# A spectral filter and a Fourier mixing layer in one kernel: new tiling of A's transform, of the slots, of B's input and of the matrix comparison

## The chip, the cores and the metric

One core of a Trainium2 chip runs the whole kernel. Its engines are PE (TensorE, matrix multiplication), DVE (VectorE), ACT (ScalarE), POOL (GpSimd) and SP (SyncE, which here only issues DMAs). Each engine works through its own list of instructions in order; semaphores join the lists. The metric is the device time of one execution in microseconds; less is better. The time before is 275.98 us, the median of three runs (274.37 to 276.39).

## The reference

Two independent layers are computed in float32 and set side by side along the last axis. S is 2048, D is 512.

```python
def _A_ref(x, w_r, w_i):
    X = rfft2(x, axes=(-2, -1))
    return irfft2(X * (w_r + 1j * w_i), s=(S, D), axes=(-2, -1))

def _B_ref(x, dft_seq_re, dft_seq_im, dft_hid_re, dft_hid_im):
    a = einsum("bsd,ed->bse", x, dft_hid_re)
    b = einsum("bsd,ed->bse", x, dft_hid_im)
    return einsum("ts,bse->bte", dft_seq_re, a) - einsum("ts,bse->bte", dft_seq_im, b)

out = concatenate([_A_ref(...), _B_ref(...)], axis=-1)
```

B's matrices are inputs: two of 2048 x 2048 (16.8 MB each) and two of 512 x 512. The kernel computes B by a fast transform, which is right only if these matrices are the Fourier matrices. So it also reads them whole and compares them with tables; if they differ, a fallback (`_b_from_c`) computes B again with the matrices as they are.

## The kernel before, in words

There are three strands of work. Python generators (`a_work`, `b_work`, `all_compared`) emit them, two lists of numbers (`B_AT`, `C_AT`) say between which steps of A the steps of B and C are emitted, and a scheduler then sets the final order of each engine.

**A, the filter.** `forward` loads x in eight pieces of 512 KB (SP), forms sums and differences of mirrored halves (DVE, `TT`, 16 of 512 elements), transforms the hidden axis in groups (PE, `hidden`: eight matmuls 256 wide for each of eight groups; the weights are every 16th column), copies to SBUF (ACT, `taken`, L489), does a first small transform along the sequence (PE, `along`: two matmuls 512 wide) and copies again (ACT, L496). Now the sequence has to become the partition. This turn goes through DRAM: POOL issues 16 DMAs of 256 KB into `out_a` as scratch (L498), and SP reads them back into `zv` in eight DMAs of 512 KB. Eight `slot`s then follow, one per residue of the sequence frequency: sums and differences (DVE), two matmuls (`px`), two multiplications of 1024 by the weights, sums and differences again, eight matmuls (`pi`, L455 with `it`) and two ACT copies back into `zv` (L600). The first frequency column is repaired by small operations on POOL (L531, L532, L581, L582), and ACT flips a sign in the weights (L521). `inverse` is two stages: 64 matmuls 256 wide out of `zv` with ACT copies (L619), then 64 matmuls 256 wide out of those with ACT copies (L630), and four stores of 1 MB.

**B, the mixing layer.** x_b is loaded in eight pieces of 512 KB of 64 partitions each, so that partition p and its mirror stand together. `b_fold` adds and subtracts mirrored columns (DVE, 8 operations of 1024). `b_along` transforms groups of 16 rows (PE, 128 matmuls of 128 or 72 columns; three ACT copies per group). `b_hidden` transforms the hidden axis (nine times, five matmuls each), `b_rows` the rest of the sequence (eight times). Each row block goes out twice, by a direct and an indirect DMA, both issued by POOL (L442, L443).

**C, the comparison.** `compare` loads 64 blocks of 512 KB of the matrices into three buffers (`raw`, SP, L323) and, for each, writes the difference to the table `tt` in bfloat16 (`diff`, DVE, L309 with a sign per partition or L311). ACT then takes the absolute value of each pair and sums it (L302, 34 of 2048 elements). The sum is compared with a threshold (L711), SP reads the flag, and a branch decides on the fallback.

PE has one list for all three, and so has DVE; all matmuls of A are recorded at L455 and all tensor_tensor operations of DVE at L226, whatever emits them.

Of the kernel before, what the change touches and what calls it, by code (L numbers as in the profile page):

```python
# [18 lines left out]
YB = 2  # L19
RAW = 3  # L20


B_AT = [4, 10, 10, 12, 12, 14, 14, 14, 14, 15, 15, 15, 15, 17, 19, 19, 19, 19, 26, 28, 30, 32, 35, 38, 40, 42]
C_AT = [0, 0, 0, 0, 0, 0, 0, 0, 0, 0, 0, 0, 0, 0, 0, 0, 0, 0, 0, 0, 0, 6, 6, 6, 6, 6, 35, 35, 35, 35, 35, 35, 35, 35, 35, 35, 35, 35, 35, 35, 35, 35, 35, 35, 35, 35, 35, 35, 37, 37, 37, 37, 37, 37, 37, 37, 37, 37, 37, 37, 37, 37, 37, 37, 37, 37, 37, 37]
SMALL = 2.0**-27

# [26 lines left out]
def _seq_order():  # L55

    j = np.arange(64)
    return ((128 * np.arange(16)[:, None, None] + np.stack([j, -1 - j])) % S).reshape(-1)
# [8 lines left out]
def _tables_b():  # L67
# [22 lines left out]

    rows = _b_rows()
# [25 lines left out]
    return fb.reshape(2, 128, 128).transpose(1, 0, 2), mb, hc  # L117


def _tables():  # L120
# [17 lines left out]
    inv = fwd.transpose(0, 3, 2, 1)  # L138
    inv0 = (fwd0 * np.array([1, 1, -1, -1])[:, None, None, None]).transpose(3, 0, 2, 1)

    th = _ang(np.outer(np.arange(S // 2), np.arange(513)), S)
    tt = np.stack([np.cos(th), -np.sin(th)]).reshape(2, 4, 2, 128, 513).transpose(1, 0, 3, 2, 4)
# [3 lines left out]
    fb, mb, hc = _tables_b()  # L146
    j = np.arange(128)
    place = np.stack([j, np.where(j, 256 - j, 128)])
# [6 lines left out]
    a = np.arange(8)[:, None] + 8 * np.arange(2)  # L155
    f16 = np.zeros((8, 2, 8, 16, 8))
    for k in range(16):
        th = _ang(a * (k // 2), 16)
        re, im = (np.cos(np.pi * a) if k == 1 else np.cos(th)), -np.sin(th)
        top, low = (re, re) if k < 2 else (im, -re) if k % 2 else (re, im)  # L160
        for n in range(4):
            f16[:, :, n, k, n] = f16[:, :, 4 + n, k, n] = top
            f16[:, :, n, k, 4 + n] = low
            f16[:, :, 4 + n, k, 4 + n] = -low
    back = np.where((np.arange(16) % 2 == 1) & (np.arange(16) > 1), -1.0, 1.0)[:, None, None, None, None]
    g16 = (f16.transpose(3, 4, 1, 0, 2) * back).reshape(128, 128)
    g16 = np.concatenate([g16, -g16], 1)

    di = np.zeros((128, 2, 2, 2, 128))
    for h in range(2):  # L170
# [8 lines left out]
    turn = (S - _b_rows()).T % S  # L179
    turn[0, 0] = S // 2  # L180
    return {
        "fwd": fwd.reshape(7, 128, 128).astype(np.float32),
        "fwd0": fwd0.reshape(4, 128, 128).transpose(1, 0, 2).reshape(128, 512).astype(np.float32),
        "inv": inv.reshape(7, 128, 128).astype(np.float32),
        "inv0": inv0.reshape(128, 512).astype(np.float32),
        "hf": hf.reshape(2, 128, 512).transpose(1, 0, 2).astype(np.float32),
        "f16": f16.reshape(128, 128).astype(np.float32),
        "g16": g16.astype(np.float32),
        "di": di.reshape(128, 1024).astype(np.float32),
        "tt": tt.astype(np.float32),  # L190
        "ht": ht.astype(np.float32),
        "odd": odd.astype(np.float32),
        "fb": fb.astype(np.float32),
# [7 lines left out]
def kernel(  # L201
# [13 lines left out]

# [7 lines left out]
    def STT(*args, **kw):  # L228
        last[0] = nc.vector.scalar_tensor_tensor(*args, **kw)

# [3 lines left out]

    ap = first.enter_context(tc.tile_pool(name="ap", bufs=1))
    bp = first.enter_context(tc.tile_pool(name="bp", bufs=1))  # L240
    rp = first.enter_context(tc.tile_pool(name="rp", bufs=2, side="right"))
# [3 lines left out]
    def region(name):  # L245

        return ap.tile([P, 8208 if name == "big" else 8192], F32, name=name)

    def part(v, kb, *shape):

        v = v[:, 256 * kb : 256 * kb + math.prod(shape)]
        if len(shape) == 1:
            return v
        names = "abcde"[: len(shape)]
        return v.rearrange("p (%s) -> p %s" % (" ".join(names), " ".join(names)), **dict(zip(names, shape)))
# [3 lines left out]
    ht = bp.tile([P, 2, 2, 257], F32, name="ht")  # L259
    hc = bp.tile([P, 2, 257], F32, name="hc")  # L260
    fb = bp.tile([P, 2, 8, 16], F32, name="fb")
    mb = bp.tile([P, 1409], F32, name="mb")
    ye = bp.tile([P, 2304], F32, name="ye").rearrange("p (j c s) -> p j c s", c=2, s=9)
    yo = bp.tile([P, 128, 25], F32, name="yo")
    stat = bp.tile([P, 34], F32, name="stat")
    ones = bp.tile([P, P], F32, name="ones")
    odd = bp.tile([P, 2], F32, name="odd")
    turn = bp.tile([P, 8], mybir.dt.int32, name="turn")
    nc.gpsimd.dma_start(turn, tabs["turn"])
    nc.vector.memset(ones, 1.0)  # L270

    zero = bp.tile([P, 2, 1024], mybir.dt.bfloat16, name="ec", bufs=2)[:, 0, :512]
    nc.vector.memset(zero, 0.0)
    warm = ps_a.tile([P, 2, 512], F32, name="pa")
    for _ in range(9):
        nc.tensor.matmul(warm[:, 0], zero[:, :P], zero, start=True, stop=True)

    loads = []

    def load(dst, src):  # L280
        loads.append(nc.sync.dma_start(dst, src))
        return dst

    def late(dst, src):

        with tc.issue_after(loads[-1].ins):
            nc.sync.dma_start(dst, src)

    tt, hts = {}, []
    pin = [None]  # L290

    def table(pr, m):

        if (pr, m) not in tt:
            tt[pr, m] = bp.tile([P, 2, 513], F32, name="tt", bufs=3)
            nc.sync.dma_start(tt[pr, m], tabs["tt"][pr, m])
        return tt[pr, m]

    def compared(i, d):

        flat = d.rearrange("p m i -> p (m i)")
        nc.scalar.activation(flat, flat, mybir.ActivationFunctionType.Abs, accum_out=stat[:, i : i + 1])  # L302

    def diff(out, raw, v, flip, sign):

        with tc.issue_after(pin[0].ins) if pin[0] is not None else ExitStack():
            if sign is not None:
                k = int(sign != flip)
                nc.vector.scalar_tensor_tensor(out, v, odd[:, k : k + 1], raw, op0=MUL, op1=SUB)  # L309
            else:  # L310
                nc.vector.tensor_tensor(out=out, in0=raw, in1=v, op=ADD if flip else SUB)  # L311

    def compare():

        i = 0
        for pr in (0, 4, 1, 5, 2, 6, 3, 7):
            for tb in range(4):
                d = bp.tile([P, 2, 1024], mybir.dt.bfloat16, name="ec", bufs=2)
                for m in range(2):
                    t = table(pr % 4, m)  # L320
                    v = t[:, :, 512:0:-1] if tb % 2 else t[:, :, :512]
                    raw = bp.tile([P, 2, 512], F32, name="raw", bufs=RAW)
# [8 lines left out]
                    if m == 1:  # L331
                        compared(i, d)
                        i += 1
                    yield 1.2

    def hidden_table():

# [494 lines left out]
```

## Time and profile before

| what | value |
|---|---|
| time, median of 3 runs | 275.98 us |
| the profiled execution: span from first to last instruction | 276.3 us |
| granted TensorE clock, mean | 0.850 |
| PE, DVE, ACT, POOL busy | 211.5, 161.2, 136.0, 42.8 us |
| DMA | 73.85 MB, mean 267 GB/s |
| matmuls of the first stage of the inverse | 195.90 to 226.4 us |
| flag written | 270.25 us |

The profile is one execution recorded by hardware. The span is the profiled execution's own time; it is 0.1% over the median of the runs. A row of the grouped lines reads: line, engine, operation, output and inputs with their shapes, count, then busy time, mean ns of one, and the idle time of the engine ahead of these instructions with what ended it. A row of a timeline reads: start, duration, engine, line, operation, count, and in brackets the idle time before it and its releaser. A row of the stretches reads: the stretch, busy time and count for PE, PE's weight loads, DVE, ACT and POOL, the granted clock, the share of the DMA engines and GB/s. A row of the chain reads: start, duration, what. An f32 matmul leaves two records on PE, so x16 there are eight instructions.

### The profile page before, as it was taken

What the parts mean: (1) busy time and instruction counts of PE and PEld (TensorE: products, weight loads), DVE (VectorE), ACT (ScalarE), POOL (GpSimd) and SP (SyncE); (2) the same over time, 40 slices, a digit from 0 to 9 for tenths busy, and PEclk for the clock granted to TensorE, in tenths of its full rate; (3) what the DMA queues carried; (4) which work ended last, traced back from release to release, by engine and by line L of the source; (5) the groups of instructions that cost most, each with busy time, mean ns of one, the idle gap of its engine ahead of it and who ended that gap; (6) DMA issues with size and microseconds to landing.
All of it is one profiled execution on the core that took longest, in us unless ns stands there. A gap on an engine that the chain in (4) does not pass through costs nothing.

```text
span 276.3 us, 2713 instructions
## 1 busy us (share of the span) xinstructions
PE 211.5 (77%) x833; PEld 169.0 (61%) x833; DVE 161.2 (58%) x225; ACT 136.0 (49%) x219; POOL 42.8 (15%) x80
## 2 busy tenths in 40 slices
PE   5049999299878799999999676302999995999630
PEld 1039788177678358787875445002799994876520
DVE  0860001685748359797968679745485754675340
ACT  1001430649866251856337235415678775774570
POOL 3000120013210016250213333013010100000000
PEclk9658999899955599999999797755599999899795
DMA  7999999889995998585844343775979888889763
GB/s 256 403 243 214 215 379 418 293 267 343 354 401 181 367 399 311 193 248 194 289 145 109 141 161 103 288 250 208 284 250 332 298 259 294 273 279 369 287 264 126
DMA packets 27460, 73.85 MB, mean 267 GB/s; under 512 B 2928, under 2 KB 9072, under 8 KB 26928
## 3 DMA queue, kind: packets, MB, share of 16 engines
q1 hardware_dynamic: 24432, 64.48, 70.5%
q0 software_dynamic: 2720, 8.56, 8.2%
q10 hardware_dynamic: 288, 0.59, 0.7%
q8 instruction: 8, 0.13, 0.2%
q14 instruction: 12, 0.10, 0.1%
HBM read 61.03 MB, written 12.58 MB: 266 GB/s over the span
## 4 chain that ended last, share of the span: by engine, by line
DMA 48%; PE 24%; DVE 13%; issue 8%; ACT 4%; SPq 1%; POOL 0%; DVEq 0%; POOLq 0%; ACTq 0%
DMA raw<-in_cm 23%; PE pa L455 12%; DMA ht<-tab_ht 6%; DMA out_b<-yb,turn 6%; DMA big<-in_xb 6%; DVE ec L309 5%; PE pb L414 4%; DVE ec L311 3%; PE pb L412 3%; DMA zv<-in_xa 2%; DMA zv<-out_a 2%; ACT ec L302 2%; DMA out_b<-yb 2%; DVE yb L226 2%; DVE sda L226 2%
## 5 line engine op out<-in xcount | busy, mean ns | idle before, releaser
L302 ACT ACTIVATE ec<-ec 128x2048 bf16<-128x2048 bf16 x34 | 65.0, 1911 | 33.4 <-DVE ec L311 21.8
L311 DVE TENSOR_TENSOR ec<-raw,tt 128x512 bf16<-128x512 f32 (+1 forms) x48 | 40.0, 865 | 51.7 <-DMA raw<-in_cm 51.6
L309 DVE SCALAR_TENSOR_TENSOR ec<-tt,odd,raw 128x512 bf16<-128x512 f32 (+1 forms) x48 | 42.5, 926 | 19.2 <-DMA raw<-in_cm 18.9
L455 PE MATMUL pa<-zb,sda 128*128 128x256 f32 x128 | 32.2, 410 | 12.2 <-DVE sda L226 12.2
L455 PEld LDWEIGHTS pa<-zb,sda 128*128 128x128 f32 x128 | 30.4, 307 | 15.5 <-DVE sda L226 13.1
L455 PE MATMUL pa<-ye,sda 128*128 128x256 f32 x128 | 32.2, 414 | 6.5 <-ACT zb L630 3.4
L455 PEld LDWEIGHTS pa<-ye,sda 128*128 128x128 f32 x128 | 26.4, 208 | 12.2 <-ACT zb L630 4.6
L455 PE MATMUL pa<-it,sda 128*128 128x128 f32 x112 | 19.2, 339 | 17.9 <-POOL sda L581 16.0
L455 PEld LDWEIGHTS pa<-it,sda 128*128 128x128 f32 x112 | 17.9, 246 | 23.6 <-POOL sda L581 20.1
L455 PE MATMUL pa<-ye,zv 128*128 128x256 f32 x128 | 30.5, 403 | 0.7 <-ACT zv L600 0.7
L455 PEld LDWEIGHTS pa<-ye,zv 128*128 128x128 f32 x128 | 29.3, 306 | 1.8 <-ACT zv L600 1.0
L226 DVE TENSOR_TENSOR sda<-zv 128x512 f32<-128x512 f32 x30 | 19.5, 687 | 15.4 <-DMA zv<-in_xa 7.5
L226 DVE TENSOR_TENSOR sda<-sda 128x512 f32<-128x512 f32 (+1 forms) x34 | 23.0, 717 | 0.3
L489 ACT COPY zb<-pa 128x1024 f32<-128x1024 f32 x8 | 8.1, 1007 | 28.5 <-PE pa L455 28.5
L226 DVE TENSOR_TENSOR sda<-pa,sda 128x1024 f32<-128x1024 f32 (+1 forms) x16 | 17.7, 1151 | 5.6 <-ACT sda L557 3.9
L455 PE MATMUL pa<-zb 128*128 128x512 f32 x32 | 16.6, 645 | 5.5 <-ACT zb L489 5.5
L397 PE MATMUL pb<-fb,yb 128*128 128x72 f32 x64 | 14.5, 319 | 3.1 <-ACT ye L403 3.1
L397 PEld LDWEIGHTS pb<-fb,yb 128*128 128x128 f32 x64 | 13.1, 248 | 6.2 <-ACT ye L403 4.0
L397 PE MATMUL pb<-fb,big 128*128 128x128 f32 (+1 forms) x64 | 16.5, 351 | 0.0
L498 POOL DMA_DIRECT2D out_a<-zb x16 | 8.5, 534 | 49.5 <-ACT zb L496 49.3
L429 ACT COPY yb<-pb 128x514 f32<-128x514 f32 x8 | 4.7, 587 | 19.4 <-DMA out_b<-yb,turn 17.1
L397 PEld LDWEIGHTS pb<-fb,big 128*128 128x128 f32 x64 | 13.1, 251 | 1.0 <-issue 1.0
(78 smaller groups left out, 247.0 us busy)
## 6 DMA issues: line engine op xcount, KB each, us to landing
raw<-in_cm SPq DMA_DIRECT2D x64, 512.0 KB, 4.9
tt<-tab_tt SPq DMA_DIRECT2D x8, 513.0 KB, 10.3
zv<-in_xa SPq DMA_DIRECT2D x8, 512.0 KB, 8.6
big<-in_xb SPq DMA_DIRECT2D x8, 512.0 KB, 16.1
out_a<-zb POOLq DMA_DIRECT2D x16, 256.0 KB, 6.2
sda<-in_wa SPq DMA_DIRECT2D x16, 256.0 KB, 3.4
zv<-out_a SPq DMA_DIRECT2D x8, 512.0 KB, 8.7
out_a<-zb SPq DMA_DIRECT2D x4, 1024.0 KB, 6.9
```

Source lines behind the costliest of these rows:

```text
L226: last[0] = nc.vector.tensor_tensor(**kw)
L302: nc.scalar.activation(flat, flat, mybir.ActivationFunctionType.Abs, accum_out=stat[:, i : i + 1])
L309: nc.vector.scalar_tensor_tensor(out, v, odd[:, k : k + 1], raw, op0=MUL, op1=SUB)
L311: nc.vector.tensor_tensor(out=out, in0=raw, in1=v, op=ADD if flip else SUB)
L397: nc.tensor.matmul(bank[:, at : at + n].rearrange("p (j s) -> p j s", j=8), v[:, cols], f[:, :, k], start=True, stop=True)
L412: nc.tensor.matmul(out, yo[0:1, :, at[1]], hc[0:1, 1], start=False, stop=True)
L414: nc.tensor.matmul(bank[:, 257:], yo[:, :, at[2] + 16 * c], ht[:, c, 1, 1:256], start=c == 0, stop=c == 1)
L429: nc.scalar.copy(y[:, :, :257], bank[:, :257].unsqueeze(1).to_broadcast([P, 2, 257]))
L455: mma[0] = nc.tensor.matmul(*args, **kw)
L489: nc.scalar.copy(zs[p], pd[p])
L498: nc.gpsimd.dma_start(bounce[:, 2 * p + k], ys[:, k])
```

## The change

Everything but the launch and the fallback is written anew.

- **A's x and the turn.** x_a goes into blocks of 8 KB per partition (`blk`). Six such blocks are shared by x_a, x_b and the matrices of C (`NB = 6`). DVE forms sums and differences in 8 operations of 1024. A group's weights are contiguous. The turn no longer goes through DRAM: after each group's second copy ACT issues two DMAs (L306) that move 256 KB from SBUF to SBUF, from 128 partitions of `work` to 8 partitions of `zv`.
- **Slots** are taken in the order 1, 2, 0, 3 to 7. Each has two sums of 512, one copy of 4 columns, one multiplication of 2048, four sums of 512 and one small multiplication by a sign, all on DVE; POOL keeps only the copy of four weight columns. The forward and inverse tables come in one load (`fi`).
- **The inverse** goes by halves of four groups of rows: eight matmuls 256 wide (L406), one ACT copy of 1024 (L408), eight matmuls 128 wide (L412), one ACT copy of 512 (L414) and two sums on DVE. Four stores of 1 MB follow, each of all 512 rows.
- **B's x is not folded.** ACT copies the mirrored columns to `xr` (L478, L479), and each group is 4 matmuls (200 or 144 wide) that accumulate x's part and xr's, then one ACT copy (L488). The direct stores of the row blocks are issued by ACT (`put`), the indirect ones by POOL.
- **C** loads 1 MB at a time into a block and compares it in one DVE operation of 2048 elements, exactly (not_equal), with the count of differences written to `stat`. The tables are scaled by a power of two. ACT's 34 passes go; ACT flips signs of a table four times. The flag asks for a count of zero.
- **The order** is written as "a9 b8 a60 b20 c": steps of A, B and C as they are emitted. The scheduler still sets the final order.

The core of the diff:

```diff
-        bounce = out_a.rearrange("d s -> (d s)").rearrange("(s g j f) -> s g j f", s=16, g=16, j=8)
...
-                        mm(pd[p][:, k, 256 * h : 256 * h + 256],
-                           u[:, h, r].rearrange("p i b -> p (i b)")[:, 2 * p + k :: 16], hf[:, r, h], start=r == 0, stop=r == 1)
+                            mm(out, u[:, h, c, k, 128 * r : 128 * r + 128], hf[:, k, h], start=k == 0, stop=k == 1)
...
-            for k in range(2):
-                nc.gpsimd.dma_start(bounce[:, 2 * p + k], ys[:, k])
-        rows = bounce.rearrange("s g j f -> (g j) s f")
-        for e in range(8):
-            nc.sync.dma_start(zv[:, 2 * e : 2 * e + 2], rows[:, 2 * e : 2 * e + 2])
+                for r in range(2):
+                    at = _place(8 * r + i, 0)
+                    nc.scalar.dma_start(zv[at : at + 29 : 4], ys[:, r])
...
+        TT(out=m.rearrange("p i (r q) f -> p i r (q f)", r=2), in0=x2, in1=w2, op=MUL)
...
+                            mm(pu[:, j, h], gz[:, 32 * q + 16 * h + g :: 64], di[:, h, q], start=q == 0, stop=q == 1)
+                u = part(1024 * (half % 2), 2, 4, 128)
+                nc.scalar.copy(u, pu.rearrange("p j h (k n) -> p j (h k) n", k=2))
+                po = ps_a.tile([P, 2, 2, 2, 128], F32, name="pa")
+                for j in range(2):
+                    for q in range(4):
+                        mm(po[:, j, q // 2, q % 2], u[:, j, q], g16, start=True, stop=True)
+                sc = part(2048 + 512 * (half % 2), 2, 2, 128)
+                nc.scalar.copy(sc, po[:, :, 1])
+                for r, op in enumerate((ADD, SUB)):
+                    TT(out=ob[:, r, :, 2 * half : 2 * half + 2].rearrange("p k j s -> p j k s"),
+                       in0=po[:, :, 0], in1=sc, op=op)
...
+                for c, (at, w) in enumerate(((0, 200), (200, 144))):
+                    lo = 128 * c
+                    mm(bank[:, at : at + w], x[:, g, lo : lo + 128], fb[:, n // 15, 0, :w], start=True, stop=False)
+                    mm(bank[:, at : at + w], xr[:, g, lo : lo + 128], fb[:, n // 15, 1, :w],
+                       start=False, stop=True)
+                nc.scalar.copy(yall[:, :, 8 * n : 8 * n + 8], bank[:, :344].rearrange("p (s j) -> p s j", j=8))
...
-        nc.scalar.activation(flat, flat, mybir.ActivationFunctionType.Abs, accum_out=stat[:, i : i + 1])
+            nc.vector.scalar_tensor_tensor(raw, raw, k, v, op0=MUL, op1=ALU.not_equal, accum_out=stat[:, i : i + 1])
...
-    nc.vector.tensor_scalar(flag, pf, SMALL, None, op0=ALU.is_le)
+    nc.vector.tensor_scalar(flag, pf, 0.0, None, op0=ALU.is_equal)
```

The change moves instructions at three places that the steps of the prediction touch. The first is the start of ACT's list. DMAHW0 to DMAHW7 are the eight semaphores that SP's and ACT's DMAs use in turn. Before, ACT's first rows are these, with the forward's copies (L489, L496) alone:

```order
L468 DMA zb<-tab_hf 128x1024
L469 DMA zb<-tab_f 128x128
L489 ACT_TABLE_LOAD
L489 COPY zb<-pa 128x1024 x2
L496 COPY zb<-pa 128x1024
```

In the change the copies are L298 and L303, and the turn's DMAs stand between them:

```order
L298 COPY work_83<-pa_116 128x1024 [waits PE_49]
L303 COPY work_83<-pa_126 128x1024 [waits PE_49]
L306 DMA zv_82<-work_83 8x16x512 [waits DMAHW7_49,Activation_49]
L306 DMA zv_82<-work_83 8x16x512 [waits DMAHW1_49]
L298 COPY work_83<-pa_132 128x1024 [waits PE_49]
L303 COPY work_83<-pa_142 128x1024 [waits PE_49]
```

The DMAs that hold these two semaphores ahead of ACT's are in SP's list, the ones with DMAHW7 and DMAHW1 at x_b's third and fourth quarter (`blk_338`, `blk_368`):

```order
L464 DMA blk_275<-in_xb 64x4x512 [waits DMAHW0_49]
L467 DMA blk_275<-in_xb 64x4x512 [waits DMAHW1_49]
L473 DMA hc_106<-tab_hc 128x514 [waits DMAHW2_49]
L474 DMA ht_107<-tab_ht 128x1028 [waits DMAHW3_49]
L475 DMA mb_109<-tab_mb 128x1409 [waits DMAHW4_49]
L464 DMA blk_308<-in_xb 64x4x512 [waits DMAHW5_49]
L467 DMA blk_308<-in_xb 64x4x512 [waits DMAHW6_49]
L464 DMA blk_338<-in_xb 64x4x512 [waits DMAHW7_49,DVE_49]
L467 DMA blk_338<-in_xb 64x4x512 [waits DMAHW0_49]
L464 DMA blk_368<-in_xb 64x4x512 [waits DMAHW1_49,DVE_49]
```

The turn's issue moved from POOL's list into ACT's, between the copies of one group and the next.

The second place is DVE's list around the compares and the slots. Before, the list goes on like this behind the last sums of the slots, with compares (L309, L311) and the last of B's rows (`yb<-yb,pb`):

```order
L311 TENSOR_TENSOR ec<-raw,tt 128x1024 x2
L226 TENSOR_TENSOR yb<-yb,pb 128x255 x2
L309 SCALAR_TENSOR_TENSOR ec<-tt,odd,raw 128x1024 x4
L311 TENSOR_TENSOR ec<-raw,tt 128x1024 x2
L311 TENSOR_TENSOR ec<-raw,tt 128x512 x4
L309 SCALAR_TENSOR_TENSOR ec<-tt,odd,raw 128x512 x8
```

In the change the first 16 compares stand ahead of the first slot (`work<-zv`), with two of B's rows between them:

```order
L563 SCALAR_TENSOR_TENSOR blk,stat<-blk,odd,tt 128x2048
L228 TENSOR_TENSOR yb<-yb,pb 128x255 x2
L563 SCALAR_TENSOR_TENSOR blk,stat<-blk,odd,tt 128x2048
L563 SCALAR_TENSOR_TENSOR blk,stat<-blk,tt 128x2048
L228 TENSOR_TENSOR yb<-yb,pb 128x255 x2
L563 SCALAR_TENSOR_TENSOR blk,stat<-blk,tt 128x2048
L563 SCALAR_TENSOR_TENSOR blk,stat<-blk,odd,tt 128x2048 x2
L563 SCALAR_TENSOR_TENSOR blk,stat<-blk,tt 128x2048
L228 TENSOR_TENSOR work<-zv 128x512 x4
L333 COPY work<-zv 128x4
```

The other 16 stand between the operations of the slots, the flag's row stands ahead of the last slots' sums, and behind the last slot only the inverse's 16 sums are left.

The third place is the end of PE's list, the inverse. Before, its two stages stand one behind the other:

```order
L455 MATMUL pa<-it,sda 128x128 x8
L422 MATMUL pb<-big,mb 128x512 x2
L455 MATMUL pa<-it,sda 128x128 x8
L455 MATMUL pa<-ye,zv 128x256 x64
L455 MATMUL pa<-ye,sda 128x256 x64
L710 MATMUL pb<-rs,ones 128x1
```

In the change they alternate, eight times in all (the first of them here), behind the last slots' matmuls (L338 `px`, L382 `pi`):

```order
L618 MATMUL pb<-rs,ones 128x1
L382 MATMUL pa<-fi,work 128x128 x8
L338 MATMUL pa<-work,fi 128x512 x2
L382 MATMUL pa<-fi,work 128x128 x16
L406 MATMUL pa<-ta,zv 128x256 x8
L412 MATMUL pa<-ta,work 128x128 x8
```

The flag's matmul (`rs,ones`) moved from behind the inverse to ahead of it.

More of the change, by code (lines that the diff above doesn't have):

```diff
@@ L275 @@
     for _ in range(9):
[L276 to L297, printed above, removed]
```

746 lines of the change are left out of this document (342 added, 404 removed).

## The prediction

> **What bounds the kernel now.** I read the page first (span, busy shares, the chain that ended last), then the chain in order of time, then the timeline of each engine in the stretches that the chain names.
>
> ```profile
> span 276.3 us, 2713 instructions
> PE 211.5 (77%) x833; PEld 169.0 (61%) x833; DVE 161.2 (58%) x225; ACT 136.0 (49%) x219; POOL 42.8 (15%) x80
> DMA 48%; PE 24%; DVE 13%; issue 8%; ACT 4%; SPq 1%; POOL 0%; DVEq 0%; POOLq 0%; ACTq 0%
> ```
> ```profile
> 86.97 5.34 DMA zv<-out_a
> ...
> 104.92 0.78 PE pb L412 x2
> 105.70 1.26 PE pb L414 x4
> 107.88 0.78 PE pb L412 x2
> ...
> 180.37 8.30 DMA out_b<-yb,turn
> ...
> 193.92 6.34 DMA raw<-in_cm
> ```
> No engine is full. There are four stages. Loads and A's forward end with the last read-back from out_a (86.97 + 5.34 = 92.3 us). From there to about 150 us the chain runs on PE, with B's hidden transforms one every 107.88 - 104.92 = 2.96 us. Then B's indirect stores hold it. From 194 us on it is the loads of cm, 512 KB each, while PE does the inverse beside them. What counts for the change is that last stage: today DVE's compares and PE's inverse share the last 80 us. The sum below is made against the span, 276.3 us; the median of the runs, 275.98, is 0.1% under it, and about 1% is what a measurement of this kernel can tell from no change.
>
> **The turn moves to ACT's queue, behind B's loads.** The eight DMA semaphores (lanes) go round over all of SP's and ACT's DMAs, and each DMA waits for the last one on its lane. In the order of the change, ACT's first two turn DMAs (L306, group 0) wait for lanes that SP's loads of x_b hold: the first halves of quarters 2 and 3 (L464). What such a wait looks like is in the trace of now:
> ```profile
> 0.74 5.87 SPq L281 DMA_DIRECT2D zv<-in_xa  x8
> 7.73 9.56 SPq L281 DMA_DIRECT2D big<-in_xb  x8
> 18.89 0.34 SPq L375 DMA_DIRECT2D hc<-tab_hc  x1
> 21.36 0.33 SPq L339 DMA_DIRECT2D ht<-tab_ht  x1
> 23.77 0.32 SPq L377 DMA_DIRECT2D mb<-tab_mb  x1
> 26.21 0.32 SPq L296 DMA_DIRECT2D tt<-tab_tt  x1
> ```
> SP's 17th DMA and those after it go out one at a time, 2.43 us apart, as the x_b loads eight places ahead of them land (18.89 to 26.21 is three steps of 2.44; 512 KB in 2.43 us is 216 GB/s). An engine whose queue holds its next instruction behind such a DMA does nothing else meanwhile, as POOL shows:
> ```profile
> 189.22 0.56 POOL L442 DMA_DIRECT2D out_b<-yb  x1 [7.86 <-DMA out_b<-yb,turn]
> 190.90 0.49 POOL L581 COPY sda<-sda 128x2 f32<-128x2 f32 x1 [1.12 <-DVE sda L226]
> ```
> POOL stood 7.86 us for a landing, and the small copy of a slot ran behind it. Now the same happens to ACT: behind its second turn DMA stands the copy of group 1 (L298), which PE's next matmul needs, and behind that everything of A's forward and B's first transforms.
>
> When are the loads there? The rates are these:
> ```profile
> 10.00:20.00 10.00, 2.48 (x6) 2.04 (x7) 8.16 (x16) 0.00 (x0) 0.00 (x0) 0.50 1.04 307
> 40.00:50.00 10.00, 8.28 (x34) 7.10 (x33) 1.68 (x2) 0.49 (x1) 1.05 (x2) 1.00 1.02 413
> ```
> x_a and the first table are 4.8 MB at the 300 to 307 GB/s of the start: 16.5 us. Two slots' weights and tables and fb are 1.72 MB, 4.2 us at 413 GB/s, 8.0 at 216: taken 5.5, so 22.0. Then quarter 0 (2 x 2.43 = 4.9), hc, ht and mb (1.51 MB at 413: 3.7), quarters 1 and 2 (4 x 2.43 = 9.7), and the first half of quarter 3 (2.4). ACT is free at **42.7 us**; 35 if all of it ran at 413, 45 with the slow end of the small loads.
>
> **PE from there.** The prices per instruction:
> ```profile
> 17.52 9.75 PE L455 MATMUL pa<-zb,sda 128*128 128x256 f32 x32 [12.16 <-DVE sda L226]
> 27.10 1.88 PE L455 MATMUL pa<-zb 128*128 128x512 f32 x4
> 28.82 3.67 PE L455 MATMUL pa<-zb,sda 128*128 128x256 f32 x16
> ...
> 163.55 2.05 PE L455 MATMUL pa<-it,sda 128*128 128x128 f32 x16 [1.75 <-POOL sda L581]
> ...
> 191.44 3.78 PE L455 MATMUL pa<-it,sda 128*128 128x128 f32 x16 [11.20 <-POOL sda L581]
> 195.90 30.47 PE L455 MATMUL pa<-ye,zv 128*128 128x256 f32 x128 [0.68 <-ACT zv L600]
> ```
> Each f32 matmul leaves two records, so a group of eight 256 wide costs 3.67, two of 512 cost 1.88, one of 128 costs 2.05 / 8 = 0.256, and between 0.256 and 0.459 lie 0.37 for 200 wide and 0.28 for 144. That the weights are now contiguous changes nothing: the 256-wide matmul already takes its full time with strided ones. Ahead of the first slot in PE's order stand, from the hold on: six along pairs and group 1's (7 x 1.88 = 13.2), six forward groups (22.0), B's 64 matmuls (32 x 0.65 = 20.8; today 128 of them), four hidden (4 x 2.95 = 11.8), and two rows (five of 257 for row 0, 2.3, and one of 512, 0.9). That is 71.0. To it come the copy and DMA that are held (1.5), a cold clock after 20 us of idleness (9.75 - 2 x 3.67 = 2.4, as at 17.52) and hand-overs to ACT's copies (3.5): 121.1. Behind it, ACT's copy (0.6), DVE's two adds (0.75) and four compares, which stand in DVE's order between row 1 and the first slot (9.6, below): the first slot's add begins at **132 us**.
>
> **DVE from there.** In the order of the change nothing follows the slots but the inverse's sums; all that remains of the compares is woven in before the last slots. The rows:
> ```profile
> L309 DVE SCALAR_TENSOR_TENSOR ec<-tt,odd,raw 128x512 bf16<-128x512 f32 x32 | 22.3, 747 | 14.2 <-DMA raw<-in_cm 14.1
> L309 DVE SCALAR_TENSOR_TENSOR ec<-tt,odd,raw 128x1024 bf16<-128x1024 f32 x16 | 20.2, 1283 | 5.0 <-DMA raw<-in_cm 4.9
> L226 DVE TENSOR_TENSOR sda<-pa,sda 128x1024 f32<-128x1024 f32 x14 | 16.5, 1217 | 1.7 <-POOL sda L582 1.7
> L226 DVE TENSOR_TENSOR yb<-yb,pb 128x255 f32<-128x255 f32 x16 | 6.0, 415 | 11.5 <-ACT yb L429 11.5
> L302 ACT ACTIVATION_READ_ACCUMULATOR ec<-ec 128x1 f32 x34 | 6.4, 190 | 0.0
> L619 ACT COPY sda<-pa 128x1024 f32<-128x1024 f32 x8 | 8.0, 1004 | 2.0 <-PE pa L455 2.0
> ```
> ```profile
> 7.81 2.50 DVE L226 TENSOR_TENSOR sda<-zv 128x512 f32<-128x512 f32 x4 [6.49 <-DMA zv<-in_xa]
> ```
> ```profile
> 260.19 2.74 DVE L309 SCALAR_TENSOR_TENSOR ec<-tt,odd,raw 128x512 bf16<-128x512 f32 x4 [5.00 <-DMA raw<-in_cm]
> ...
> 270.25 0.16 DVE L711 TENSOR_SCALAR flag<-pb 128x1 int32<-128x1 f32 x1 [0.68 <-PE pb L710]
> ```
> From 512 to 1024 elements a compare grows by 0.536 us, so 2048 cost 1.283 + 1.072, less 0.05 where one follows the next (four of 512 take 2.74, not 4 x 0.747): 2.31. It now also sums into stat; DVE has no such row. ACT's read of its sum costs 0.19; the bounds are 0 and 0.19, and I take 0.1: 2.41. After 132 us DVE has 16 compares (38.6), 8 hidden ones (8 x 0.79 = 6.3), 8 multiplies of 2048 (1.217 + 1.06 - 0.06 = 2.22, 17.8), 48 adds of 512 (30.2 at 2.50 / 4), 12 row adds (4.5), 16 small ones at 0.16 (2.6) and the flag (0.35): 100.4, with 3.5 for waits on PE and the table's sign flips on ACT. The last slot leaves DVE at **236 us**. ACT is rid of 34 passes of 1.9 us and POOL of its part in the slots; neither is on this path.
>
> The Trainium skill (VectorE: DVE Perf Modes, "Two Vector instructions with no wait between them") says that an operation which writes out its accumulator is two instructions, the main one and an accumulator read. ACT's row of 190 ns agrees for ACT, and no row of now shows DVE; by it the sum would be 2 us longer.
>
> **The inverse and the end.** Today 64 matmuls of the first stage run in one go (30.47 us) and 64 of the second follow, beside compares. Now each of eight halves is eight matmuls of 256, a copy of 1024, eight of 128, one behind the other on PE, since the 128-wide ones wait for the copy and the next half stands behind them: 3.81 + 1.00 + 0.1 + 2.05 = 6.96, times eight 55.7. PE's work is less than now (46.9 against 62.7), but nothing runs beside it. Ahead stand the last slot's eight matmuls and two copies: 195.90 - 191.44 = 4.5, taken 5; bounds 3.3 and 10. Behind stand a copy (0.6), two adds (1.3) and the store:
> ```profile
> out_a<-zb SPq DMA_DIRECT2D x4, 1024.0 KB, 6.9
> ```
> 0.6 + 1.3 + 6.9 and 1.2 for the end: 10. So 236 + 5 + 55.7 + 10 = 306.7: I say **306 us**, 11% over now. With the hold's end between 35 and 45, the sum's read between 0 and 0.19 and the step ahead of the inverse between 3.3 and 10, this case alone lies between 296 and 316.
>
> **Rivals.** *The hold is not there (other side).* If the lanes that ACT waits for are free when it comes to them, PE goes on at 20 us. It decides whether ACT's second turn DMA goes out before about 25 us. PE then needs 20.3 + 71.0 + 7.4 and reaches row 1's adds at about 100, and the 16 compares' own loads (18.9 MB at 413 behind x_b's 43 us, and the turn's 4.2 MB) at 99 to 103; the slots start at 103, and 103 + 100.4 + 3.5 + 5 + 55.7 + 10 = **278 us**, no change, with 270 to 284 about it by the unknown prices, the lower part faster than now. For it: the turn is no longer two passes through DRAM, and POOL's queue had no hold in the forward. Against it: the row of the 17th DMA shows that lanes are waited for.
>
> *The turn is slow.* Each turn DMA writes 8 partitions. If the 4.2 MB go at 216 GB/s, as x_b's 64 partitions do, and not 413, they need 19.4 us of the queues and not 10.2. The last of them lands then up to 9 us later; about 12 us lie between its landing at some 120 us and the first slot at 132, so most is hidden. Where several are queued up behind cm's loads, the slots start 10 us later: **316 us**. The Trainium skill (DMA: Bandwidth & Descriptors, "Why a DMA increments its semaphore by 16 and not by 1") has a DMA use the largest number of engines up to 16 that divides the slowest dimensions of both sides; for 8 and 128 that would be 8 engines, half of them. No DMA of now writes 8 partitions, so no row bears it out or speaks against it.
>
> *The new compare finds a difference.* It is for exact equality where the old one had a threshold; then the fallback runs and adds more than 100 us. Nothing in the profile speaks for it.
>
> **How the numbers follow.** The held case has 0.55, the case without the hold 0.25 (0.11 faster by over 1%, 0.09 within, 0.05 slower), the slow turn 0.13, the fallback 0.03, and 0.04 stand for other delays, all slower. So faster 0.11, same 0.09, slower 0.80. The range that holds 8 in 10 reaches from 273, into the second case, to 320, over the third.
>
> **What would show it.** Right: ACT idle from about 18 to 43 us, ended by the landing of blk<-in_xb, with PE idle beside it; the first add on zv at about 132 us; DVE over 95% busy from there to 236; the inverse's first L406 at about 241, and PE idle for 1.1 us ahead of each L412. Wrong: group 1's L298 copy at 21 us; compares well under 2.3 us; the first slot much before 125 us with DVE not full behind it; or B's stores, now on ACT's queue, holding ACT's copies again.

## The result, and the profile after

The changed kernel takes **321.15 us** (median of 4 runs, 320.22 to 322.24); the kernel before, beside it on the same chip, 276.19 us. The ratio is 1.163, with a 95% interval from 1.155 to 1.170: 16% slower. The forecast was 306 us, with a range from 273 to 320. The direction and the stages are as forecast; the time is 15 us above the forecast and 1 us above its range. The profiled execution has a span of 318.4 us, 0.9% under the median.

The page of the changed kernel, first its span, the busy shares, then the chain by engine:

```profile
span 318.4 us, 2428 instructions
PE 201.8 (63%) x849; PEld 149.8 (47%) x849; DVE 152.5 (48%) x199; ACT 72.5 (23%) x114; POOL 28.0 (9%) x25
...
PE 39%; DMA 28%; DVE 18%; ACT 5%; issue 5%; SPq 3%; ACTq 0%; DVEq 0%
```

Every engine does less than before (ACT 72.5 us against 136.0, PE 201.8 against 211.5, DVE 152.5 against 161.2), the DMAs move 70.35 MB against 73.85, and the kernel takes 42 us longer. So the loss is in waits. Stage by stage, the forecast beside the profile:

| point | forecast | profiled |
|---|---|---|
| ACT gets past its second turn DMA | 42.7 | 42.4 to 43.1 |
| first slot's add on DVE | 132 | 141.7 |
| last slot leaves DVE | 236 | 248.6 |
| first matmul of the inverse | 241 | 253.3 |
| last matmul of the inverse | 296.7 | 308.2 |
| end | 306.7 | 318.4 |

The start of ACT's list in the timeline (start, duration, engine, line, operation, count, and in brackets the idle time and its releaser):

```profile
15.14 1.01 ACT L298 COPY work<-pa 128x1024 f32<-128x1024 f32 x1 [12.71 <-PE pa L296]
18.23 1.01 ACT L303 COPY work<-pa 128x1024 f32<-128x1024 f32 x1 [2.07 <-PE pa L301]
37.55 5.53 ACTq L306 DMA_DIRECT2D zv<-work  x2
43.12 1.01 ACT L298 COPY work<-pa 128x1024 f32<-128x1024 f32 x1 [23.88 <-DMA blk<-in_xb]
```

Between its copies of group 0 and of group 1 ACT does nothing for 23.88 us, and what ends it is the landing of an x_b load, which has nothing to do with the turn. PE's list shows the same time (one row, the first matmul behind it):

```profile
44.18 3.74 PE L301 MATMUL pa<-work,ta 128*128 128x512 f32 x4 [22.54 <-ACT work L298]
```

A second stand of the same kind comes later, which the forecast did not have. ACT's rows, then PE's, then one of SP's:

```profile
111.56 1.01 ACT L303 COPY work<-pa 128x1024 f32<-128x1024 f32 x1 [1.57 <-DMA zv<-work]
113.28 9.72 ACTq L306 DMA_DIRECT2D zv<-work  x2
123.04 0.62 ACT L528 COPY yb<-yb 128x510 f32<-128x510 f32 x1 [10.47 <-DMA zv<-work]
```
```profile
124.10 1.22 PE L497 MATMUL pb<-hc,yall 128*128 128x257 f32 x2 [10.40 <-ACT yb L535]
```
```profile
97.18 9.59 SPq L578 DMA_DIRECT2D blk<-in_cm  x4
```

The two DMAs are the turn of the last group. They wait for the lanes of two 1 MB loads of cm out of SP's row. By the semaphores in the trace these are the first load of that row, which lands at 113.20 us, and the third, which lands at 122.35; ACT's two DMAs go out at 113.28 and 122.37. (The releaser in ACT's next row, zv<-work, is inferred from the same semaphore, which ACT's own second DMA is the next to use.) Behind them in ACT's list stand the copies of B's row 0, which PE waits for. The first slot's add follows late:

```profile
141.71 2.49 DVE L228 TENSOR_TENSOR work<-zv 128x512 f32<-128x512 f32 x4
```

DVE from the first slot on, by stretches (stretch, then busy time and count of PE, PE's weight loads, DVE, ACT, POOL, the granted clock, the share of the DMA engines, GB/s):

```profile
141.70:160.00 18.30, 6.57 (x8) 2.52 (x8) 17.56 (x38) 1.35 (x3) 0.00 (x0) 0.64 1.01 401
160.00:200.00 40.00, 15.99 (x56) 10.31 (x56) 39.97 (x45) 6.85 (x12) 18.50 (x6) 0.67 0.94 337
200.00:220.00 20.00, 17.64 (x74) 11.94 (x74) 18.42 (x27) 7.15 (x14) 1.64 (x3) 0.76 0.22 74
220.00:238.40 18.40, 10.92 (x37) 6.56 (x37) 12.69 (x24) 4.49 (x8) 3.23 (x4) 0.78 0.22 86
238.40:248.60 10.20, 6.73 (x32) 5.03 (x30) 5.04 (x6) 2.15 (x4) 0.61 (x1) 0.81 0.07 26
...
253.30:308.20 54.90, 45.72 (x256) 43.15 (x256) 9.02 (x14) 12.19 (x15) 0.00 (x0) 1.00 0.15 58
```

From 141.7 to 200 us DVE is full (57.5 of 58.3 us) while PE idles more than half the time. From 200 us on the DMAs fall to 74 GB/s; at 214.5 us the last compare is through, and the slots go on as a chain of waits between DVE and PE. In the inverse (253.3 to 308.2) little but PE and its copies runs: DVE is busy 9 of 55 us. Before, DVE's compares and the loads of cm filled that stretch. PE's rows there show the stand at each copy:

```profile
301.16 3.79 PE L406 MATMUL pa<-ta,zv 128*128 128x256 f32 x16
306.11 2.05 PE L412 MATMUL pa<-ta,work 128*128 128x128 f32 x16 [1.16 <-ACT work L408]
```

### The profile page after: what moved, and what is told of

Same layout as the page of the kernel before. It is cut to its first block, busy times and chain, and to the rows that moved or that the text cites. A ratio compares the mean times of both kernels' runs of the same rounds, so it can differ in the third digit from the quotient of the medians.

```text
span 318.4 us, 2428 instructions
## 1 busy us (share of the span) xinstructions
PE 201.8 (63%) x849; PEld 149.8 (47%) x849; DVE 152.5 (48%) x199; ACT 72.5 (23%) x114; POOL 28.0 (9%) x25
## 2 busy tenths in 40 slices
DMA packets 30002, 70.35 MB, mean 221 GB/s; under 512 B 1936, under 2 KB 11024, under 8 KB 29472
## 4 chain that ended last, share of the span: by engine, by line
PE 39%; DMA 28%; DVE 18%; ACT 5%; issue 5%; SPq 3%; ACTq 0%; DVEq 0%
DMA blk<-in_cm 13%; DVE work L228 11%; PE pa L406 9%; DMA blk<-in_xb 8%; DVE blk L563 6%; PE pa L412 5%; PE pa L296 4%; DMA zv<-work 4%; PE pa L382 4%; PE pa L338 3%; PE pa L301 3%; ACT work L408 3%; DMA blk<-in_xa 2%; PE pb L485 2%; PE pb L501 2%
## 5 line engine op out<-in xcount | busy, mean ns | idle before, releaser
L563 DVE SCALAR_TENSOR_TENSOR blk<-blk,tt 128x2048 f32<-128x2048 f32 (+2 forms) x24 | 41.6, 1754 | 25.8 <-DMA blk<-in_cm 18.2
L563 DVE SCALAR_TENSOR_TENSOR blk<-blk,odd,tt 128x2048 f32<-128x2048 f32 x16 | 37.2, 2346 | 5.4 <-DMA blk<-in_cm 5.4
L296 PE MATMUL pa<-ta,work 128*128 128x256 f32 x128 | 31.2, 400 | 3.9 <-DVE work L228 3.9
L296 PEld LDWEIGHTS pa<-ta,work 128*128 128x128 f32 x128 | 25.9, 203 | 11.7 <-DVE work L228 4.8
L406 PE MATMUL pa<-ta,zv 128*128 128x256 f32 x128 | 30.5, 391 | 1.2 <-ACT zv L387 1.2
L406 PEld LDWEIGHTS pa<-ta,zv 128*128 128x128 f32 x128 | 28.8, 304 | 1.5 <-ACT zv L387 1.5
L382 PE MATMUL pa<-fi,work 128*128 128x128 f32 x112 | 18.1, 328 | 10.4 <-DVE work L228 10.4
L382 PEld LDWEIGHTS pa<-fi,work 128*128 128x128 f32 x112 | 17.6, 241 | 12.7 <-issue 12.5
L412 PE MATMUL pa<-ta,work 128*128 128x128 f32 x128 | 16.4, 281 | 9.1 <-ACT work L408 9.1
L338 PE MATMUL pa<-work,fi 128*128 128x512 f32 x28 | 18.2, 793 | 5.5 <-DVE work L333 4.4
L412 PEld LDWEIGHTS pa<-ta,work 128*128 128x128 f32 x128 | 14.9, 191 | 11.5 <-ACT work L408 11.5
L298 ACT COPY work<-pa 128x1024 f32<-128x1024 f32 x8 | 8.1, 1013 | 53.2 <-PE pa L296 29.4
L301 PEld LDWEIGHTS pa<-work,ta 128*128 128x128 f32 x32 | 6.0, 206 | 30.2 <-ACT work L298 25.8
L228 DVE TENSOR_TENSOR work<-work 128x512 f32<-128x512 f32 x32 | 20.1, 680 | 0.1
```

What stands on the lines that cost most here:

```text
L228: last[0] = nc.vector.tensor_tensor(**kw)
L296: mm(out, u[:, h, c, k, 128 * r : 128 * r + 128], hf[:, k, h], start=k == 0, stop=k == 1)
L301: mm(y[:, r], f16, zs[:, r], start=True, stop=True)
L338: mm(flat(px[:, i]), ft[:, 0], flat(t[:, i]), start=True, stop=True)
L382: mm(pi[:, i, q], lhs[i], it[:, 0], start=True, stop=True)
L406: mm(pu[:, j, h], gz[:, 32 * q + 16 * h + g :: 64], di[:, h, q], start=q == 0, stop=q == 1)
```

## The experiments

Each kernel below was timed in 3 rounds beside the kernel before on its chip; that took 276.7 to 277.0 us in all of them but the last (275.9). L is the theory of the prediction: three losses, ACT held at DMA issues, compares between the slots, and an inverse in which PE stands at each copy.

**e1: the turn issued by POOL.**

```diff
-                    nc.scalar.dma_start(zv[at : at + 29 : 4], ys[:, r])
+                    nc.gpsimd.dma_start(zv[at : at + 29 : 4], ys[:, r])
```

> The turn's 16 DMAs are issued by POOL and not by ACT; all else as changed. Theory (ACT stands at its own DMA issues for lanes that SP's loads hold, 24 us at 18 us and 10 us at 112 us): both idle stretches of ACT go, PE goes on at about 20 us, the first slot's add on zv comes at 103 to 112 us and not 141.7, and the time is 280 to 292 us. Rival (the loads pace the first 140 us whoever issues the turn): the first slot stays after 130 us and the time over 308. Rival (a turn DMA that writes 8 partitions is slow by itself): ACT is free, but the first add on zv waits for zv's landing beyond 125 us.

Measured: 294.95 us, ratio 1.065 (1.058 to 1.072), 26 us less than the changed kernel. ACT goes straight on:

```profile
18.53 1.01 ACT L303 COPY work<-pa 128x1024 f32<-128x1024 f32 x1 [2.07 <-PE pa L301]
21.98 1.01 ACT L298 COPY work<-pa 128x1024 f32<-128x1024 f32 x1 [2.44 <-PE pa L296]
```

```profile
117.82 2.50 DVE L228 TENSOR_TENSOR work<-zv 128x512 f32<-128x512 f32 x4
```

The first slot's add comes at 117.8 us, 24 us earlier, but not at 103 to 112, and the time is 3 us over what L expects: who issues the turn costs 26 us, and of the 34 us that ACT stood, 10 are taken back by something else. ACT's waits from 10 to 142 us in this kernel (engine, line, what it waited for: us in total, times, longest) name one candidate, and the stretches of this kernel the other:

```profile
ACT tt L574 <- DVE blk L563: 11.1, 1, 11.1
```
```profile
65.00:79.00 14.00, 6.05 (x32) 5.43 (x32) 9.32 (x8) 2.86 (x7) 1.19 (x2) 0.88 1.03 400
79.00:118.00 39.00, 28.21 (x96) 17.02 (x96) 28.86 (x29) 12.91 (x22) 5.03 (x7) 0.89 1.03 403
```

ACT stands at the sign flip of a table (L574) until DVE has done the fourth compare, with two forward copies behind it; and from 65 us on the loads of cm run at 400 GB/s without a gap. e13 bears on this.

**e11 and e10: each of ACT's two stands alone.**

```diff
-                    nc.scalar.dma_start(zv[at : at + 29 : 4], ys[:, r])
+                    (nc.gpsimd if i < 4 else nc.scalar).dma_start(zv[at : at + 29 : 4], ys[:, r])
```

is e11; e10 has `i >= 6` in place of `i < 4`.

> The changed kernel, with the turn's DMAs of the last two groups alone issued by POOL; ACT keeps the first six groups and with them its first hold (18 to 42 us). Theory (the 10 us by which the first slot came later than forecast are ACT's second hold, at the last group's DMA behind 1 MB loads of cm): the first hold stays, ACT's stand at 113 to 122 us goes, the first slot comes at about 132 us as forecast, and the time is 309 to 314 us. Rival (cm's loads set the first slot at 141 us, and the hold lies beside them): under 4 us less, over 317.

> The changed kernel, with the turn's DMAs of the first four groups alone issued by POOL; ACT keeps the last four and with them its second hold. Theory (both holds cost, and without the first one the loads of cm pace what follows, as in e1): PE goes on at 20 us, ACT still stands some 10 us at the last group, the first slot comes at 120 to 130 us, the time is 298 to 309. Rival (only the second hold costs, since the loads take back what the first one frees): over 315.

Measured: e10 310.98 us (ratio 1.128, 1.118 to 1.139), 10.2 us less than the changed kernel; e11 306.69 us (1.113, 1.104 to 1.122), 14.5 less. Together 24.7, near e1's 26.2. The first slot's add in e10 and in e11:

```profile
135.12 2.49 DVE L228 TENSOR_TENSOR work<-zv 128x512 f32<-128x512 f32 x4
```
```profile
126.67 2.49 DVE L228 TENSOR_TENSOR work<-zv 128x512 f32<-128x512 f32 x4
```

e10 keeps the first stand (ACT waits 24.7 us for blk<-in_xb) and loses the second: its first slot starts 6.6 us earlier than the changed kernel's, 3 us behind the forecast's 132, and the whole time is 10 us less. So the second stand, which the forecast did not have, is worth 10 us: 6.6 up to the first slot, and the rest in a shorter stretch of slots (103.1 us and not 106.9; why was not followed up). What holds e10's first slot beyond 132 are cm's loads: the compares ahead of it now wait for them, as in this row.

```profile
130.32 2.35 DVE L563 SCALAR_TENSOR_TENSOR blk<-blk,odd,tt 128x2048 f32<-128x2048 f32 x1 [2.05 <-DMA blk<-in_cm]
```

In e11 the second stand is still there (its pair takes 7.75 us to issue), and the first slot comes 15 us earlier: the first stand, 24 us long, is worth 14.5.

**e3: the same move in the kernel before.**

```diff
-                nc.gpsimd.dma_start(bounce[:, 2 * p + k], ys[:, k])
+                nc.scalar.dma_start(bounce[:, 2 * p + k], ys[:, k])
```

> The kernel before, with one edit: the 16 DMAs of its turn into DRAM are issued by ACT and not by POOL. Theory (hold by lanes): ACT's second copy of the forward is held until x_b's loads land, from about 29 us to 36 or 40 us, PE's forward ends some 8 us later and the time goes up by 3 to 10 us (280 to 286). Rival (who issues the turn does not matter, since the loads bound that stretch): no change, 274 to 278.

Measured: 285.62 us, ratio 1.030 (1.024 to 1.036), 9 us more. ACT's row shows the stand:

```profile
28.47 1.01 ACT L496 COPY zb<-pa 128x1024 f32<-128x1024 f32 x1 [0.70 <-PE pa L455]
43.26 3.06 ACTq L498 DMA_DIRECT2D out_a<-zb  x2
46.36 1.01 ACT L489 COPY zb<-pa 128x1024 f32<-128x1024 f32 x1 [16.88 <-DMA raw<-in_cm]
```

ACT stood 16.88 us, longer than expected, and 9 of them show in the time. The lanes were not held by x_b's loads, as expected, but by loads issued behind these: by the semaphores in the trace, of a table and of cm (35.95 to 45.74 us). This one edit, with nothing else of the change, makes the old kernel 3% slower; the rival of no change is out.

**e5: the second half of the compares behind the slots.**

```diff
+        slots_done.append(last[0])
...
                         unequal(i, raw, v, k)
                         i += 1
+                        if i == LATE_FROM:
+                            pin[0] = slots_done[LATE_SLOT]
```

with 16 and -1: `pinned()` then puts compares 17 to 32 and the hidden ones behind the last slot's last operation on DVE.

> The changed kernel, with compares 17 to 32 and the hidden ones that follow them in the program put behind the last slot's last DVE operation, so that they run beside the inverse. Theory (DVE is full from the first slot to the last, so the 16 compares of 2.4 us that stand between the slots' operations are on the path): the inverse starts 25 to 38 us earlier, and the time is 285 to 298. Rival (the slots are a chain DVE, PE, DVE, ACT, with compares filling its gaps): less than 15 us, over 306.

Measured: 289.62 us, ratio 1.049 (1.044 to 1.054), 31.5 us less than the changed kernel, in the middle of what L expects. The first matmul of the inverse stands at 220.70 us and not 253.3, and DVE's compares now lie beside it (PE's row, then two rows of DVE's timeline, the first compare and one in the midst of the inverse's sums):

```profile
220.70 5.52 PE L409 MATMUL pa<-ta,zv 128*128 128x256 f32 x16 [1.16 <-ACT zv L390]
```
```profile
216.36 0.69 DVE L567 SCALAR_TENSOR_TENSOR blk<-blk,tt 128x514 f32<-128x514 f32 x1
...
247.28 2.34 DVE L567 SCALAR_TENSOR_TENSOR blk<-blk,odd,tt 128x2048 f32<-128x2048 f32 x1
```

So the slots' stretch was bound by DVE, and by compares that nothing needed there. The slots alone are still a chain: first add 141.07, last operation 216.45 us, 75 us against 107, with DVE idle between.

**e4: the inverse's halves overlapped.** `head(n)` holds what was taken out, the 256-wide matmuls and the ACT copy of half n:

```diff
+        head(0)
         for quad in range(4):
...
             for half in range(2):
-                pu = ps_a.tile([P, 2, 2, 256], F32, name="pa")
...
-                u = part(1024 * (half % 2), 2, 4, 128)
-                nc.scalar.copy(u, pu.rearrange("p j h (k n) -> p j (h k) n", k=2))
+                if 2 * quad + half < 7:
+                    head(2 * quad + half + 1)
+                u = us[2 * quad + half]
                 po = ps_a.tile([P, 2, 2, 2, 128], F32, name="pa")
```

> The changed kernel, with the first matmuls of the next half of the inverse emitted ahead of the second matmuls of this half, so that ACT's copy runs beside PE. Theory (PE stands 1.1 us for each of eight copies and nothing else runs there): seven of eight go, 7 to 9 us less than the changed kernel, 312 to 314. Rival (PE has slack there, the end is set by ACT or the stores): under 3 us.

Measured: 309.84 us, ratio 1.119 (1.112 to 1.125), 11.3 us less than the changed kernel, more than the 7 to 9 expected. PE's rows follow one another without a stand:

```profile
263.88 3.79 PE L405 MATMUL pa<-ta,zv 128*128 128x256 f32 x16
267.51 1.95 PE L419 MATMUL pa<-ta,work 128*128 128x128 f32 x16
```

The inverse's matmuls take 43.5 us (254.83 to 298.33) and not 54.9, so the whole gain lies there. A half takes 5.42 us and not 6.84. Not seven but all eight stands are gone, the first too, since the second half's first matmuls run beside it; at 1.10 to 1.16 us they make 9. The other 2.3 us are in the rows' overlap: without a stand, matmuls start before the row ahead of them has ended. The rival (slack on PE) is out.

**e2: the stores of B's rows on POOL too.**

```diff
-            nc.scalar.dma_start(dst, v)
+            nc.gpsimd.dma_start(dst, v)
```

> As e1 (POOL issues the turn's DMAs), and POOL issues the direct stores of B's rows too. Theory (in e1 ACT no longer stands long at a DMA issue; its waits at the stores are about 4 us in all, beside a full DVE): 0 to 4 us less than e1, 291 to 295. Rival (the stores on ACT hold the copies that the slots' path needs): 6 us or more less, under 289.

Measured: 294.98 us, ratio 1.067 (1.058 to 1.077); e1 has 294.95. With the turn gone from ACT's queue, the stores on it cost nothing that shows.

**e6 and e9: all of it together.** e6 has the edits of e2, e4 and e5; e9 those of e1, e4 and e5.

> The changed kernel with four edits: POOL issues the turn's DMAs and the direct stores of B's rows, the inverse's halves overlap, and compares 17 to 32 with the hidden ones stand behind the last slot. If the three losses (ACT's holds, compares between the slots, PE's stand at each copy of the inverse) lie behind one another on the path, their gains add up: 321 - 26 - 11 - 31 = 253; DVE then has 54 us of work beside an inverse of 48, so up to 6 more: 250 to 262, below the kernel before. Rival (the gains overlap: what one edit frees the next wait takes): over 270.

> As e6, with the direct stores of B's rows left on ACT's queue. Theory (as for e2): within 3 us of e6. Rival (with DVE no longer full between the slots, ACT's stands at the stores come onto the path): 5 us or more over e6.

Measured: e6 262.85 us, ratio 0.952 (0.937 to 0.968), e9 263.57 us, 0.954 (0.946 to 0.962). The new parts, with the waits taken out, are 5% faster than the kernel before by e6, and 4% by e13 below, whose four runs lie within 0.2 us of one another. e6's four runs are 260.5, 261.1, 264.6 and 265.3 us, so that 3 us beside it are not told apart. Its median, just above the expected 250 to 262, is 58 us under the changed kernel; the three gains by themselves (26.2, 11.3, 31.5) add to 69. What they share shows in e6's stretches:

```profile
65.00:115.00 50.00, 33.23 (x123) 21.57 (x121) 34.96 (x33) 14.54 (x23) 7.22 (x10) 0.90 1.03 403
115.00:200.00 85.00, 56.29 (x204) 36.17 (x205) 54.60 (x87) 18.57 (x36) 13.39 (x18) 0.78 0.39 142
200.00:250.00 50.00, 47.03 (x274) 46.20 (x273) 49.35 (x65) 16.63 (x22) 0.00 (x0) 0.97 0.87 336
```

From 65 to 115 us the DMAs are the bound (403 GB/s), from 115 to 200 the chain of the slots (no engine over 70%), and from 200 to 250 DVE (49.35 of 50 us), with PE nearly as full. e9 shows no cost of the stores on ACT beyond that spread.

**e8, e12 and e13: three attempts to go on from e6, without a clear gain.** e8 has 12 compares ahead of the slots, not 16. e12 is e8 with two compares each behind the second, fourth and sixth slot. e13 is e8 with the tables' sign flips on DVE, those of `tt` as shown and those of `hs` likewise:

```diff
-LATE_FROM = 16
+LATE_FROM = 12
```
```diff
+LATE_AT = {12: 1, 14: 3, 16: 5, 18: 7}
...
-                        if i == LATE_FROM:
-                            pin[0] = slots_done[LATE_SLOT]
+                        if i in LATE_AT:
+                            pin[0] = slots_done[LATE_AT[i]]
```
```diff
-                            nc.scalar.mul(t[:, :, 1::2], t[:, :, 1::2], -1.0)
+                            nc.vector.tensor_scalar(t[:, :, 1::2], t[:, :, 1::2], -1.0, None, op0=MUL)
```

> As e6, with the compares from the 13th on behind the last slot, not from the 17th. Theory (DVE beside the inverse is by now the bound of the end; the slots start when the first compares' blocks have come): the slots start up to 10 us earlier, and the end, with 20 compares and 64 us of DVE work beside 48 us of the inverse, stays where it was: within 4 us of e6. Rival (the slots' start sets the end): 8 us or more less than e6.

> As e8 (12 compares ahead of the slots, four edits), with two compares each behind the second, fourth and sixth slot, where DVE stands idle for PE, and the rest behind the last slot. Theory (in e8 DVE's work beside the inverse sets the end): 4 to 12 us less than e8, 250 to 258. Rival (the gaps between the slots' operations are too short for a compare of 2.3 us, so that each delays a slot): within 3 us of e8, over 258.

> As e8, with the sign flips of the tables on DVE and not on ACT. In e8 ACT stands 11.1 us at the first flip for DVE's fourth compare, with two copies of the forward behind it, and PE then stands 8.8 us for ACT. Theory (this is the same loss as at the turn's DMAs: an instruction that waits long, in the list of an engine that others need): PE's 8.8 us go, the first slot comes some 8 us earlier (100 us), and the time is 251 to 257 us, since the slots and DVE's work behind them shift as a whole and DVE gains 3 us of work. Rival (the loads of cm, at 403 GB/s from 65 to 115 us, pace the first slot): within 3 us of e8, over 258.

Measured: e8 261.55 us, ratio 0.946 (0.938 to 0.955), not to be told from e6; e12 264.77 us (0.960, 0.951 to 0.969); e13 265.05 us (0.958, 0.951 to 0.965). For e8 the theory holds: the slots start at 108.23 us and not 115.7, and the end stays, since DVE has that much more beside the inverse. e12 went as its rival has it: at 3.2 us over e8 the compares in the gaps did not pay, and the last slot was done at 203.6 us, in e8 at 191.0. e13 went as its rival has it, 0.5 us beyond the rival's 3 us. PE's stand for ACT (8.8 us in e8) went, and a wait for DVE took its place (PE's waits from 10 to 110 us in e13):

```profile
PE pb L507 <- DVE yb L230: 9.7, 1, 9.7
PE pa L298 <- DVE work L230: 4.2, 1, 4.2
```

The first slot came at 108.83 us as before, so taking the flip off ACT gains nothing: another chain as long takes over. In e13 DVE's row add stands behind compares that wait for cm's loads, and PE, after its 9.7 us, ran at about half speed (the matmuls of the L511 row took 2.07 us there and 1.13 in e8). In e8 the last thing that the first slot waits for is a DMA of the turn, which lands 9.1 us after its issue, among cm's loads:

```profile
108.23 2.50 DVE L230 TENSOR_TENSOR work<-zv 128x512 f32<-128x512 f32 x4 [2.91 <-DMA zv<-work]
```

In both kernels the DMA engines are full from 18 us to the first slot (401 and 402 GB/s from 65 us on). That the loads and the turn together set the first slot without ACT's stands is the reading that fits; no run took bytes away to show it.

## Where the prediction was wrong, and what in it was right

**The hold on ACT: right, and right in size.** 42.7 us was forecast from the loads ahead of it, 42.4 measured; e1 and e11 show what it costs, and e3 that the queue move alone makes such a hold.

**The first slot at 132 us: wrong by 9.7 us, and this is the step that failed.** The step took ACT's list as free behind the first hold, with 3.5 us for "hand-overs to ACT's copies". But the same rule that was used for group 0 holds for every turn DMA behind it: each takes a lane that an earlier DMA of SP or ACT had, and by 113 us SP's DMAs are 1 MB loads of cm. The last group's pair stood 9.7 us there, with B's row 0 behind it; PE stood 10.4. The prediction named such a hold only as a sign to look for, with B's stores in mind, and priced none. e10 takes this second stand away and gives 10.2 us of the 15 back.

That the first slot is late by nearly PE's 10.4 us is in part luck. The matmuls from the end of PE's stand to the end of row 1 took 6.9 us, in e10 3.6, so the stand cost 3.4 more; against that, PE's sum up to there was 3.6 us too long. And e10's first slot at 135.1 shows that 132 was 3 us early even without the stand: the compares ahead of the slot were summed without a wait for their blocks, and in e10 they wait for cm's loads. The rest of the 15 us are 2.1 in the slots and the inverse together, 2.8 between the profiled execution and the median, and 0.7 by which 306.7 was rounded down.

**DVE from the first to the last slot: right in sum (106.9 against 103.9) by luck, with two errors against each other.** DVE's work was 93.7 us (the five stretches above) and not 100.4, its waits 13.2 and not 3.5. A third of the 6.7 us less is that the sum into stat costs next to nothing:

```profile
134.95 2.35 DVE L563 SCALAR_TENSOR_TENSOR blk<-blk,odd,tt 128x2048 f32<-128x2048 f32 x1
137.22 0.08 DVE L563 DVE_READ_ACCUMULATOR blk<-blk,odd,tt 128x1 f32 x1
137.22 2.35 DVE L563 SCALAR_TENSOR_TENSOR blk<-blk,odd,tt 128x2048 f32<-128x2048 f32 x1
```

A compare starts 2.22 to 2.27 us after the one before; 2.41 was forecast, 2.4 us too much over 16. The rest is spread over the hidden compares (0.61 us apart, not 0.79), the adds and the small operations, which overlap more in a row than their single prices say (and 48 adds at 2.50 / 4 are 30.0 us, not the 30.2 summed). There is an accumulator read, as the Trainium skill has it (VectorE: DVE Perf Modes, "Two Vector instructions with no wait between them"), but of 0.08 us and beside the next operation. The waits were more because the last slots, with no compares left, are a chain from DVE to PE and back; "over 95% busy to 236" holds to 200 us only. That DVE was the bound is shown by e5.

**The inverse: right.** 54.9 us against 55.7, with 1.16 us at each copy against 1.1; e4 gives the stands back. Ahead of it 4.7 us against 5, behind it 10.2 against 10.

**The rivals.** That the hold is not there is out; but what e1 shows without the holds is also not the 278 us of that rival. It comes to 295, since the first slot, at 117.8 us, comes behind loads and compares that were put at 99 to 103. That the turn is slow by itself is right in its rate, but it did not hold the first slot. From 69 to 71.3 us it runs almost alone; by 40 slices of the 10 us from 68 on, the share of the DMA engines in tenths and the GB/s, and the queue (q10 is ACT's):

```profile
DMA  8234454555555200000000000000000000009007
GB/s 66 16 33 57 164 180 188 213 189 188 205 180 197 98 16 0 0 0 0 0 0 0 0 0 0 0 0 0 0 0 0 0 0 0 0 0 229 0 16 197
...
q10 hardware_dynamic: 259, 0.50, 16.8%
```

It moves 164 to 213 GB/s with half of the engines. That is what the rule of the Trainium skill gives for 8 partitions (DMA: Bandwidth & Descriptors, "Why a DMA increments its semaphore by 16 and not by 1"). But DVE's first add on zv began without a wait in the changed kernel, so the last landing was hidden there, as the rival's first half said. Its second half, DMAs of the turn queued up behind cm's loads, shows on ACT: two copies waited, 3.18 and 1.57 us, for such DMAs to be done with `work`; the first of them, below, waited for one issued at 79.33 us.

```profile
92.75 1.01 ACT L303 COPY work<-pa 128x1024 f32<-128x1024 f32 x1 [3.18 <-DMA zv<-work]
```

PE stood 1.17 us behind that copy; what reached the time was not measured. The fallback did not run.

## What to carry to other kernels

Before a DMA is moved to another engine's queue, look at what that DMA waits for at its issue, for every one of them and not for the first alone: the engine stands there, and everything in its list behind. Work that nothing waits for (here the compares) belongs beside the stage in which its engine is idle, not between the links of a chain on that engine. A rewrite that makes every engine's work less can still be slower; here the same parts, with the waits taken out, came to 0.952 of the kernel before.

## What the runs showed of the hardware

PE's clock fell where PE waited much: 0.64 and 0.67 were granted from 141.7 to 200 us, and 1.00 in the inverse (rows above). The same two matmuls (four records) of a hidden transform, early and late in PE's timeline of the changed kernel:

```profile
136.98 1.13 PE L501 MATMUL pb<-ht,yall 128*128 128x255 f32 x4
...
163.23 2.07 PE L501 MATMUL pb<-ht,yall 128*128 128x255 f32 x4
```

They took nearly twice as long after a wait of 9 us (9.19, ahead of the matmul at 160.10 us). Waits thus cost PE twice. Behind the second stand this is the 3.4 us above; how much of e5's gain it is, no run separates. In e4's gain it has no part, since the clock granted in the inverse was 1.00 in both kernels.
